# Moving the loads of w1, w2, w_out and u within batch 0 of a gated-attention and maxout kernel

## The chip, the core and the metric

The kernel runs on one core of a Trainium2 chip. The metric is device time in microseconds (us) of one execution, as the median over several runs. The engines that appear here are TensorE (PE: matmuls, with its weight loads PEld), VectorE (DVE), ScalarE (ACT), GpSimd (POOL), and SyncE (SP), which issues DMAs. All DMAs run on 16 DMA engines that are fed from two queues: the hardware queue q1, which SP issues (here nearly all transposes between SBUF tiles), and the software queue q0, which POOL issues (loads from HBM with a cast from fp32 to bf16, and the stores of the output). SBUF is the on-chip memory, PSUM the accumulators that PE writes.

## The reference

```python
def _attn_ref(u, v, z):                    # u, v: (8, 3072, 256); z: (8, 3072, 64)
    scores = (1.0 / S) * np.matmul(z, z.transpose(0, 2, 1))
    attn = np.maximum(scores, 0.0) ** 2
    out = np.matmul(attn, v)
    return (u * out).astype(np.float32)

def _moe_ref(x, w1, w2, w_out):            # x: (24576, 256); w1, w2: (256, 1024); w_out: (1024, 256)
    h1 = x @ w1
    h2 = x @ w2
    g = np.maximum(h1, h2)
    return (g @ w_out).astype(np.float32)
```

The attention output of all batches, flattened to 24576 rows, is the x of the second part. All arrays are fp32.

## The kernel before

**Tiling.** A batch has 3072 rows: 24 tiles of 128, in 6 groups of 4 tiles (512 rows). The scores of a batch are a symmetric 6 x 6 arrangement of blocks A[b, g, blk] (512 by 512, bf16). PE computes a block in two score pairs (`score_pair`, L220, two matmuls of 128 by 512 into two of the four PSUM tiles of the pool `mm_psum`); ACT applies the relu into a tile r_sb (L233, three buffers), and DVE squares it into the block (L241). A block below the diagonal is mostly not computed: it is the mirror of the one above, made by a DMA transpose that SP issues (`mirror`, L272). u is needed transposed too: `load_u` fetches 512 rows on POOL's queue (L190), `turn_u` transposes them on SP's queue (L196) into a tile uT, and `gate` multiplies the attention output by it on DVE (L434, two halves) into xT. z goes a similar way: `load_z` (L136), `turn_z` with two copies on DVE (L143) and a transpose on SP (L144).

**The second part.** max(x w1, x w2) w_out is computed as relu(x (w1 - w2)) w_out + x (w2 w_out). So DVE subtracts the weights once into w15_sb (L663), SP transposes w2 into w2T (L667), and PE multiplies w2T by w_out into W2o (L682), which needs w_out in SBUF. The function `ff` (L450, L464, L473) then does the work for a group.

**Batch 0.** Groups 0 to 3 of batch 0 run first, in the loop of L614. It walks over `steps_of(i)`, pairs (n, dc) of a key tile n (0 to 23) and a half dc of the model width; `attn_unit` (L288) issues two matmuls for each. For the first and last tiles of a group the order is all n of dc 0 and then all n of dc 1: group 3 starts so with its tiles 0 to 8, that is the blocks A[0, 3, 0], A[0, 3, 1] and the first tile of A[0, 3, 2], which are mirrors of blocks that groups 0, 1 and 2 computed. Score pairs are issued between the steps, up to 11 pairs ahead of need, one in four steps. After the fourth group come W2o, the ff of groups 0 and 1, and then groups 4 and 5 and the other batches, two groups at a time (L749 on).

**What sets the order.** The order of instructions is that of the program, per engine, within `tc.manual_schedule()`. In the loop, small conditions on (i, n) place the loads: i is the group, n the tile at which dc 0 has just been issued. A DMA on POOL's queue would run as soon as its buffer is free, so the loads here are held back: a memset of one element by DVE into the tile comes first (`held=True`, or L654 for the weights), and the DMA waits for that memset, thus for DVE's place in its own order. POOL and SP issue their DMAs strictly in order, so a DMA that waits holds up those behind it.

In the kernel before, on POOL's queue: u of group 1 is loaded at (0, 18), w2 and w1 at (1, 12), z of batch 1 at (1, 16), u of group 2 at (2, 1), w_out at (2, 4), the next z at (2, 14), u of group 3 at (3, 1). On SP's queue, in order: the mirror for group 2, the turn of u of group 1 (1, 16), the mirrors that group 3 reads first (three), the turn of z (2, 8), a mirror, w2T (2, 13), a mirror, the turn of u of group 2 (2, 16), and then the mirrors kept in the list `later` for groups 4 and 5.

Of the kernel before, what the change touches and what calls it, by code (L numbers as in the profile page):

```python
# [11 lines left out]
def kernel(  # L12
# [55 lines left out]
    def by_tile(x):  # L68
        return x.rearrange("(p t) d -> p t d", t=NT)
# [52 lines left out]
    def zT_pe(lo, n, engine):  # L122
        tp = mm_psum.tile([P, n, P], bf16, name="tpz", tag="mm")
        for j in range(n):
            nc.tensor.transpose(  # L125
                tp[:, j, :], zd_first(lo + j, 1).rearrange("p t h d -> p (t h d)"), ident
            )
        copy = nc.scalar.copy if engine == "act" else nc.vector.tensor_copy
        for k in range(0, n, G):
            copy(zT[:, lo + k : lo + k + G, :], tp[:, k : k + G, :])  # L130
# [53 lines left out]
    def load_u(b, g, held=False):  # L184
        un[b, g] = unat.tile([P, G, D], bf16, name="un")
        if held:
            nc.vector.memset(un[b, g][:, 0, 0:1], 0.0)
        step = 2 if b or g > 1 else G
        for k in range(0, G, step):
            nc.gpsimd.dma_start(  # L190
                out=un[b, g][:, ds(k, step), :], in_=by_tile(u[b])[:, ds(g * G + k, step), :]
            )

    def turn_u(b, g):
        t = upool.tile([P, G, KD, P], bf16, name="uT")
        nc.sync.dma_start_transpose(  # L196
            t.rearrange("p a c r -> p (a c) r"), un[b, g].rearrange("p a d -> p (a d)")
        )
        uT[b, g] = t
# [83 lines left out]
    def attn_unit(b, g, t, acc, dc, first, last):  # L283
        blk, j = divmod(t, G)
        a = A[b, g, blk]
        for half in range(2):
            rows = ds(half * R, R)
            nc.tensor.matmul(  # L288
                a.out(acc[half, dc]),
                v_at(b, t, dc)[rows],  # L290
                a.moving(rows, j),
                start=first,
                stop=last,
            )
        if dc == KD - 1 and j == G - 1:
            a.release()
# [4 lines left out]
    def drain(acc, dcs, copy=nc.scalar.copy):  # L301
        hs = {}
        for dc in dcs:
            hs[dc] = new_h()
            copy(hs[dc], acc[1, dc])
        for dc in dcs:
            nc.vector.tensor_add(hs[dc], hs[dc], acc[0, dc])
        return hs

    def drain_fast(acc, dc):  # L310
        hs = [new_h() for half in range(2)]
        nc.scalar.copy(hs[1], acc[1, dc])
        nc.vector.tensor_copy(hs[0], acc[0, dc])
        return hs
# [174 lines left out]
    w_out_sb = consts.tile([P, KF, D], bf16)  # L489
# [30 lines left out]
    def emit_pair(wait=0):  # L520
        nonlocal done
        early = done < 12
        finish = score_pair(
            *pairs[done], dve_half=1 if early and done % 3 == 0 else None, halves=done == 0
        )
        done += 1
        if wait:
            due.append((tick + wait, finish))
        else:
            finish()  # L530
# [10 lines left out]
    def steps_of(i):  # L541
        tiles, both = range(NT), range(KD)
        head = edge(i - 1) if i else 0
        tail = NT - edge(i)
        steps = [(n, dc) for dc in both for n in tiles[:head]]
        steps += [(n, dc) for n in tiles[head:tail] for dc in both]
        return steps + [(n, dc) for dc in both for n in tiles[tail:]]

    def pair_slots(i):
        return (  # L550
            [1, 3] + list(range(6, 40, 4)),
            list(range(3, 41, 4)),
            list(range(3, 41, 4)),
            list(range(0, 44, 4)),
        )[i]

    def need(b, g, n):
        most = pair_at[b, g, 2 * g]
        for t in range(n + 1):
            if t // G >= g:  # L560
                most = max(most, pair_at[b, g, t // 2] + 1)
        return most

    with tc.manual_schedule():
# [15 lines left out]
        w1_sb, w2_sb = (w.ap.rearrange("p (c f) -> p c f", c=KD) for w in (w1, w2))  # L580
        w2T_sb = w2T.ap.rearrange("p (c k r) -> p c k r", c=KD, r=P)

        def new_acc():
            return {
                (half, dc): acc_tile(2 * half + dc) for half in range(2) for dc in range(KD)
            }
# [27 lines left out]
        for i in range(PLAIN):  # L614
            b, g = groups[i]
            if i:
                acc = new_acc()
            new, slots = {}, pair_slots(i)
            for slot, (n, dc) in enumerate(steps_of(i)):
                tick += 1  # L620
                k = need(b, g, n)
                upto = max(k, min(done + 1, k + AHEAD)) if slot in slots else k
                while done < min(upto, len(pairs)):
                    emit_pair()
                if i == 0 and slot in (10, 22):
                    zT_pe(12 if slot == 10 else 20, 8 if slot == 10 else 4, "act")
                    if slot == 22:
                        for x in z_first:
                            x.release()
                attn_unit(b, g, n, acc, dc, n == 0, n == NT - 1)  # L630
                if n == NT - 1 and i < PLAIN - 1:
                    if i < 2:
                        new[dc] = drain_fast(acc, dc)
                    else:
                        new.update(drain(acc, [dc]))
                if dc:
                    continue
                if i in (1, 2) and n in (5, 8):
                    k = n // 8
                    nc.vector.tensor_add(sums[k][0], *sums[k])  # L640
                    sums[k] = sums[k][0]
                if i and n == 11:
                    gates = gate(*groups[i - 1], sums)
                if i and n in (11, 14):
                    gates.pop(0)()
                if i == 0 and n == 14:
                    turn_u(0, 0)
                if (i, n) in ((0, 18), (2, 1), (3, 1)):
                    load_u(0, i or 1, held=True)
                if i and n == (13 if i == 3 else 16):  # L650
                    turn_u(0, i)
                if (i, n) in ((1, 12), (2, 4)):
                    w_in = ((w2_sb, moe_w2), (w1_sb, moe_w1)) if i == 1 else ((w_out_sb, moe_w_out),)
                    nc.vector.memset(w_in[0][0][:, 0, 0:1], 0.0)  # L654
                    for w_sb, w in w_in:
                        nc.gpsimd.dma_start(
                            out=w_sb, in_=w.rearrange("(c p) f -> p c f", p=P)
                        )
                if later and n % 4 == 0 and (i == 3 or i and n > 12):
                    later.sort(key=lambda block: block[2])  # L660
                    mirror(*later.pop(0))
                if i == 2 and n == 16:
                    nc.vector.tensor_sub(w15_sb, w1_sb, w2_sb)  # L663
                    w1.release()
                    w2.release(after=COOL)
                if (i, n) == (2, 13):
                    nc.sync.dma_start_transpose(  # L667
                        w2T.ap.rearrange("p (k r) -> p k r", r=P), w2.ap
                    )
                if (i, n) in ((1, 16), (2, 14)):  # L670
                    load_z(1, i - 1, held=True)
                if (i, n) in ((2, 8), (3, 4)):
                    turn_z(1, i - 2)
                if (i, n) == (3, 5):
                    load_z(1, 2, held=True)
                if (i, n) == (3, 17):
                    turn_z(1, 2)
            if i == 3:
                for dc in range(KD):
                    ps = mm_psum.tile([P, D], fp32, name="w2o_ps", tag="mm")  # L680
                    for nb in range(KF):
                        nc.tensor.matmul(  # L682
                            ps,
                            w2T_sb[:, dc, nb, :],
                            w_out_sb[:, nb, :],
                            start=(nb == 0),
                            stop=(nb == KF - 1),
                        )
                    nc.scalar.copy(W2o_sb[:, dc, :], ps)
                w2T.release()  # L690
            sums = new
# [271 lines left out]
```

## Time and profile before

| | |
|---|---|
| median of 8 runs | 920.95 us (918.48 to 922.23) |
| the profiled execution | 919.7 us, span from first to last instruction 917.9 us |
| mean granted TensorE clock | 0.994 of full |
| DMA queues | q1 91.79 MB, 63.8% of the 16 engines' span; q0 52.58 MB, 32.1% |
| HBM | 59.77 MB read, 25.17 MB written |
| load of w1, w2 (512 KB each in SBUF) | 8.4 us median from issue to landing |
| load of w_out (512 KB) | 13.6 us |
| mirror transposes, L272 and L244 (240) | 4.9 us median |

All starts are in us from the beginning of the span. Group 0 begins near 9 us, group 3 ends at 72.7, and the W2o products start at 72.84 us. Busy time of an engine does not count the issue of DMAs. In the rows of a timeline a bracket gives the engine's idle time before the instruction and what ended it. A DMA's line on SP covers the wait for its inputs and for room in the queue, not the transfer itself. The DMA share counts the busy time of packets on the 16 engines and can exceed 1, since packets overlap on an engine.

### The profile page before, as it was taken

To read this page: it belongs to the slowest core of one execution; us is meant where nothing else is said; L and a number is where in the kernel's file an instruction comes from. 1 tells how busy PE (TensorE), PEld (TensorE's weight loads), DVE (VectorE), ACT (ScalarE), POOL (GpSimd) and SP (SyncE) were. 2 spreads that over 40 slices of the span, in tenths; PEclk is the share of its full clock that TensorE was granted. 3 is DMA by queue.
4 is the path that set the end of the run, shared out by engine and by line. 5 is a ranking of instruction groups with operands and counts; after the bars stand their busy time and mean duration, and the time that the engine had idled before them with its cause. 6 is when DMAs were issued, how large, how long until landed. Compare 5 with 4: busy or idle time off the path is not lost.

```text
span 917.9 us, 19381 instructions
## 1 busy us (share of the span) xinstructions
PE 901.4 (98%) x7478; PEld 519.8 (57%) x7526; DVE 722.6 (79%) x1097; ACT 601.8 (66%) x1192; POOL 160.8 (18%) x303
## 2 busy tenths in 40 slices
PE   9969999999999999999999999999999999999998
PEld 4426465564656655656556656466565564655655
DVE  6743699788997799977998879979799788995640
ACT  7946976667675666666766676766666667673445
POOL 3100221202202122021212022130230202101000
PEclk9979999999999999999999999999999999999999
DMA  9999999989989997999969999799989989988201
GB/s 177 129 184 195 174 188 157 189 151 168 195 157 155 164 175 154 179 147 173 195 112 207 140 175 182 133 199 145 175 174 143 186 158 175 157 158 148 78 24 70
DMA packets 396557, 145.61 MB, mean 159 GB/s; under 512 B 361904, under 2 KB 387632, under 8 KB 396464
## 3 DMA queue, kind: packets, MB, share of 16 engines
q1 hardware_dynamic: 359040, 91.79, 63.8%
q0 software_dynamic: 37424, 52.58, 32.1%
q8 instruction: 59, 0.97, 0.5%
q14 instruction: 34, 0.28, 0.1%
HBM read 59.77 MB, written 25.17 MB: 93 GB/s over the span
## 4 chain that ended last, share of the span: by engine, by line
PE 94%; DMA 4%; issue 1%; DVE 1%; ACT 0%; SPq 0%; ACTq 0%; DVEq 0%
PE acc L899 44%; PE o_ps L473 18%; PE d_ps L450 18%; PE s_ps L220 7%; PE o_ps L464 5%; DMA blk<-blk 3%; PE acc L288 2%; DMA uT<-un 1%; DVE blk L241 0%; ACT r_sb L233 0%; PE acc L592 0%; PE w2o_ps L682 0%; PE tpz L125 0%; SPq L196 0%; DVE xT L434 0%
## 5 line engine op out<-in xcount | busy, mean ns | idle before, releaser
L899 PE MATMUL acc<-blk,v_sb 64*128 64x512 bf16 x2208 | 450.4, 376 | 0.0
L233 ACT ACTIVATE r_sb<-s_ps 128x512 bf16<-128x512 f32 (+3 forms) x672 | 335.8, 558 | 132.2 <-PE s_ps L220 86.3
L899 PE MATMUL acc<-blk,vt 64*128 64x512 bf16 x1512 | 364.1, 376 | 0.0
L899 PEld LDWEIGHTS <-v_sb 64*128 64x128 bf16 x2208 | 176.2, 94 | 134.9 <-issue 5.9
L241 DVE TENSOR_TENSOR blk<-r_sb 128x1024 bf16<-128x1024 bf16 x257 | 172.3, 689 | 83.6 <-ACT r_sb L233 83.0
L457 ACT ACTIVATE g_sb<-d_ps 128x512 bf16<-128x512 f32 x384 | 193.3, 627 | 28.3 <-PE acc L899 17.8
L473 PE MATMUL o_ps<-w_out_sb,g_sb 128*128 128x256 bf16 x1536 | 175.5, 273 | 0.0
L899 PEld LDWEIGHTS <-vt 64*128 64x128 bf16 x1512 | 139.2, 94 | 62.5
L450 PE MATMUL d_ps<-xT,w_sb 128*128 128x512 bf16 x720 | 167.6, 379 | 2.6 <-issue 0.2
L473 PEld LDWEIGHTS <-g_sb 128*128 128x128 bf16 x1536 | 150.3, 98 | 17.4
L486 POOL DMA_DIRECT2D out_dram<-o_sb x88 | 48.2, 548 | 542.5 <-ACT o_sb L485 542.5
L485 ACT COPY o_sb<-o_ps 128x512 f32<-128x512 f32 (+1 forms) x98 | 56.4, 578 | 132.5 <-PE o_ps L473 132.5
L776 DVE TENSOR_TENSOR h_sb<-h_sb,acc 128x512 f32<-128x512 f32 x168 | 109.5, 683 | 28.3 <-ACT h_sb L780 20.9
L220 PE MATMUL s_ps<-zT 64*128 64x512 bf16 (+3 forms) x676 | 126.7, 360 | 0.1
L450 PEld LDWEIGHTS <-w_sb 128*128 128x128 bf16 x768 | 73.3, 98 | 89.3 <-issue 9.5
L344 DVE TENSOR_TENSOR blk<-blk,blk 128x2048 bf16<-128x2048 bf16 x63 | 77.2, 1225 | 3.0 <-DMA blk<-blk 0.9
L434 DVE SCALAR_TENSOR_TENSOR xT<-h_sb,uT 128x512 bf16<-128x512 f32 x96 | 62.0, 685 | 19.5 <-DMA uT<-un 18.1
L340 DVE TENSOR_TENSOR blk<-blk,blk 128x2048 bf16<-128x2048 bf16 x63 | 76.8, 1218 | 0.0
L791 DVE TENSOR_TENSOR blk<-blk,blk 128x2048 bf16<-128x2048 bf16 x63 | 76.6, 1219 | 0.0
L348 DVE TENSOR_TENSOR blk<-blk,blk 128x2048 bf16<-128x2048 bf16 x63 | 73.3, 1219 | 1.8 <-DMA blk<-blk 1.8
L190 POOL DMA_DIRECT2D un<-in_u_dram x94 | 50.3, 551 | 106.9 <-DMA uT<-un 82.0
L239 DVE TENSOR_TENSOR blk<-r_sb 128x512 bf16<-128x512 bf16 (+3 forms) x162 | 46.5, 324 | 20.1 <-ACT r_sb L233 19.1
(49 smaller groups left out, 360.3 us busy)
## 6 DMA issues: line engine op xcount, KB each, us to landing
out_dram<-o_sb POOLq DMA_DIRECT2D x88, 256.0 KB, 4.0
un<-in_u_dram POOLq DMA_DIRECT2D x92, 128.0 KB, 5.2
v_sb<-in_v_dram POOLq DMA_DIRECT2D x74, 128.0 KB, 5.3
blk<-blk SPq DMA_TRANSPOSE x240, 4.9
v_sb<-in_v_dram POOLq DMA_DIRECT2D x11, 256.0 KB, 8.8
zn<-in_z_dram POOLq DMA_DIRECT2D x21, 128.0 KB, 4.7
out_dram<-o_sb SPq DMA_DIRECT2D x6, 256.0 KB, 2.0
blk<-in_moe_w_dram POOLq DMA_DIRECT2D x2, 512.0 KB, 8.4
```

Source lines behind the costliest of these rows:

```text
L220: nc.tensor.matmul(s_ps[h][:, lo[h] :], zT[rows, z_at(b, blk * G + tiles[h]), :], zT[rows, q + lo[h] // P : q + G, :].rearrange("p t c -> ...
L233: nc.scalar.activation(o, s, AF.Relu)
L241: nc.vector.tensor_mul(a[:, k : k + 2, :], r, r)
L340: nc.vector.tensor_add(*alike(f["S1"], f["A21"], f["A22"]))
L344: nc.vector.tensor_sub(*alike(f["S2"], f["S1"], f["A11"]))
L348: nc.vector.tensor_sub(*alike(f["S3"], f["A11"], f["A21"]))
L450: nc.tensor.matmul(d_ps, w15_sb[:, kc, ts(nb, P)], xT[:, kc, :], start=(kc == 0), stop=(kc == KD - 1),)
L457: nc.scalar.activation(g_sb[:, nb, :], d_ps, AF.Relu)
L473: nc.tensor.matmul(o_ps[t // 2][:, t % 2, :], g_sb[:, nb, ts(t, P)], w_out_sb[:, nb, :], start=False, stop=(nb == KF - 1 and t % 2 == 1),)
L776: nc.vector.tensor_add(out, a, b_)
L791: nc.vector.tensor_sub(f["A12"].ap, f["A12"].ap, f["S2"].ap)
L899: mm = nc.tensor.matmul(a.out(acc[name]), w()[rows], a.moving(rows, j), start=name not in opened, stop=left[name] == 0,)
```

## The change

Three conditions of the loop move loads to other places. The load of u for group 1 goes from (0, 18) to (1, 8), that for group 2 from (2, 1) to (2, 5); that for group 3 stays at (3, 1). w2 and w1 go from (1, 12) to (0, 18), and w_out from (2, 4) to (2, 12). Each load takes its DVE memset along. The order of PE, ACT and SP is the same as before; on POOL the two weight loads trade places with the load of u of group 1, and the other loads keep their order.

```diff
-                if (i, n) in ((0, 18), (2, 1), (3, 1)):
-                    load_u(0, i or 1, held=True)
+                if (i, n) in ((1, 8), (2, 5), (3, 1)):
+                    load_u(0, i, held=True)
                 if i and n == (13 if i == 3 else 16):
                     turn_u(0, i)
-                if (i, n) in ((1, 12), (2, 4)):
-                    w_in = ((w2_sb, moe_w2), (w1_sb, moe_w1)) if i == 1 else ((w_out_sb, moe_w_out),)
+                if (i, n) in ((0, 18), (2, 12)):
+                    w_in = ((w2_sb, moe_w2), (w1_sb, moe_w1)) if i == 0 else ((w_out_sb, moe_w_out),)
                     nc.vector.memset(w_in[0][0][:, 0, 0:1], 0.0)
                     for w_sb, w in w_in:
                         nc.gpsimd.dma_start(
                             out=w_sb, in_=w.rearrange("(c p) f -> p c f", p=P)
                         )
```

## The prediction

> **What bounds the kernel now.** I read the page first. TensorE (PE) is busy nearly all the span, so a change off PE can only win where PE stands idle or runs at a lower clock. By stretches of 10 us, PE is full from 90 us on; the loss lies between 40 and 70 us, where batch 0 runs its third and fourth query group (columns: span, PE, PE weight loads, VectorE (DVE), ScalarE (ACT), GpSimd (POOL), each busy us and instructions; granted clock; DMA share; GB/s).
>
> ```profile
> PE 901.4 (98%) x7478; PEld 519.8 (57%) x7526; DVE 722.6 (79%) x1097; ACT 601.8 (66%) x1192; POOL 160.8 (18%) x303
> ...
> 20.00:30.00 10.00, 9.61 (x92) 5.06 (x91) 7.39 (x13) 8.69 (x17) 0.54 (x1) 1.00 0.47 67
> 30.00:40.00 10.00, 9.36 (x86) 4.61 (x84) 7.11 (x16) 8.19 (x16) 3.92 (x6) 1.00 1.05 170
> 40.00:50.00 10.00, 8.89 (x82) 4.41 (x78) 9.03 (x17) 9.42 (x19) 0.54 (x1) 1.00 1.48 136
> 50.00:60.00 10.00, 3.67 (x22) 1.40 (x24) 2.98 (x9) 2.45 (x5) 1.59 (x3) 0.71 1.33 173
> 60.00:70.00 10.00, 10.00 (x74) 4.57 (x73) 2.20 (x4) 6.49 (x12) 0.00 (x0) 0.78 1.23 206
> ```
>
> DMA is half idle at 20 to 30 us and overbooked from 40 on. PE's timeline names what it waits for: three mirrored blocks, which group 3 reads first (idle time and releaser in brackets).
>
> ```profile
> 50.33 1.04 PE L288 MATMUL acc<-blk,v_sb 64*128 64x512 bf16 x8 [1.44 <-DMA blk<-blk]
> ...
> 55.99 1.89 PE L288 MATMUL acc<-blk,v_sb 64*128 64x512 bf16 x8 [4.41 <-DMA blk<-blk]
> ...
> 59.90 1.89 PE L288 MATMUL acc<-blk,v_sb 64*128 64x512 bf16 x8 [1.59 <-DMA blk<-blk]
> ```
>
> Eight matmuls take 1.89 instead of 1.04 us there: the clock was granted at half after the longest idle time. Narrow stretches show it at 0.50 from 54.3 to 64.4 us and at 1.00 again from 64.6.
>
> ```profile
> 54.30:57.60 3.30, 1.61 (x8) 0.65 (x9) 0.50 (x3) 0.00 (x0) 0.53 (x1) 0.50 1.35 188
> ...
> 61.00:64.40 3.40, 3.40 (x18) 1.41 (x16) 0.69 (x1) 1.13 (x3) 0.00 (x0) 0.50 1.23 259
> ```
>
> So the loss on PE is 1.44 + 4.41 + 1.59 = 7.4 us of waiting, and of the clock: 56.0 to 64.5 at half speed, less 1.6 idle, is 6.9 us of work that needs 3.45: together 10.9 us. Group 3 at full clock is 96 accumulating and 22 score matmuls, two at a time at 0.2155 us (eight take four such steps, 0.86): 12.7 us, from 48.9 to 61.6 instead of 72.7. But the chain of waits shows a second chain that ends at the same place:
>
> ```profile
> 31.60 28.25 DMA blk<-blk x2
> ...
> 66.05 4.66 DMA uT<-un
> ...
> 70.80 0.10 DVE xT L434
> ...
> 71.41 0.69 DVE blk L241
> ...
> 72.19 0.61 ACT r_sb L233
> ...
> 72.84 1.91 PE w2o_ps L682 x16
> ```
>
> The transpose of u of group 2 (uT2), tenth on SP's queue since 28 us, lands at 70.71; DVE's gate waits for it, the next square, the next relu, and PE's w2o products start 2.13 us after the landing, 0.16 us after PE was free. Whoever removes only the mirrors' waits gains nothing: **uT2 has to land earlier too**.
>
> **The change part by part.** PE, ACT and SP keep their order; DVE keeps its three one-element memsets (0.06 us each) and POOL its DMA issues. What moves is when loads enter the software queue (q0), which shares the DMA engines with SP's transposes (q1).
>
> ```profile
> 20.72 0.54 POOL L190 DMA_DIRECT2D un<-in_u_dram  x1 [11.72 <-DVE un L187]
> 31.01 1.41 POOL L656 DMA_DIRECT2D blk<-in_moe_w_dram  x2 [9.75 <-DVE blk L654]
> ...
> 39.05 0.89 POOL L656 DMA_DIRECT2D w_out_sb<-in_moe_w_out_dram  x1 [1.25 <-DVE w_out_sb L654]
> ```
>
> *w1 and w2 go from 31.0 to 20.7 us.* At 31 they land 7.2 and 9.6 us after issue, and of the 1.54 MB that DMA moves from 33 to 42.4 us the transposes get 0.22: the first mirror, issued at 31.60, lands at 50.28. At 20.7 only uT0 is on q1, landed at 21.4; u took 3.6 us there for 256 KB, so 1024 KB land by about 28 and hold up nobody: the next transpose issue ends at 30.2. The edit costs nothing; were that cover gone, it would delay that one mirror, which PE first reads at 36.9.
>
> *u of group 1 goes from 20.7 to about 29.0* (its memset now follows the addition that ends at 28.9). Alone 3.6 us, beside the mirror that lands at 32.60 some 5: it lands at 33 to 34. SP's uT1, issued at 30.3 until now, waits for that, and behind it in order stand the three mirrors, which start near 35 instead of 31.6. Without w1 and w2 beside them they land, at the 2.4 us that consecutive mirrors are apart from 61 to 68 us (63.22, 65.66, 68.03), near 40, 43 and, with u2 beside it, at most 49. PE wants them at 48.9, 50.0 and 51.0. uT1 itself lands near 38; its gate stands at 43.96. Price on PE: nothing, with 2 us of margin at the tightest.
>
> *u of group 2 goes from 36.7 to about 39.5*, two issues of 0.54 us. uT2 is only reached after eight other transposes: nothing. u of group 3 stays.
>
> *w_out goes from 39.05 to about 45.5* (DVE's first gate half of group 2 ends at 44.65, one square follows, then the memset). This is the edit with a price, because w_out is now ahead of a small load that DVE waits for soon. In the trace w_out lands at 52.69; u before it on q0 landed at 45.42, so its service took 7.3 us. z, issued at 46.76, followed at 55.75, 3.06 us later, and DVE waited for it, while PE stood idle anyhow:
>
> ```profile
> 55.84 0.49 DVE L143 COPY zd<-zn 128x512 bf16<-128x512 bf16 x2 [2.42 <-DMA zn<-in_z_dram]
> ```
>
> After the change w_out's packets start at about 46.8 (u's began about 1.3 us after its issue at 20.72), so w_out ends near 54.3 and z near 57.4. DVE's copy is in order at group 3's fifth tile, and the squares of later score pairs stand behind it. PE can go on for five pairs: three buffers of r_sb, and two pairs of the four PSUM tiles. At one pair in 1.08 us the first pair behind the copy is issued at 50.9 and the sixth at 56.2; from z's landing to a free PSUM tile are 0.5 (copies) + 0.7 (square) + 0.6 (relu) = 1.8 us. So z is in time until 54.4, and PE **loses about 3 us** at 56. Bounds: 0 if w_out is served at the 0.13 MB/us of the w loads' stretch (landing before 51), 8 if it takes its whole 13.6 us again.
>
> *When does uT2 land?* By megabytes left at 46.8 us. Before, q1 moved 3.37 MB from there to 70.7, q0 0.89; the last stretch, with q0 empty, ran at 0.198 MB/us:
>
> ```profile
> q1 hardware_dynamic: 13404, 3.37, 99.6%
> q0 software_dynamic: 1298, 0.89, 31.5%
> ```
> ```profile
> q1 hardware_dynamic: 7315, 1.84, 120.0%
> ```
>
> After, q1 still has w2T and two mirrors (3 x 0.524), uT2 (0.262), zT and half of the third early mirror (0.50): 2.34 MB, a lead of 1.03 MB, worth 5.2 us at 0.198. Against it q0 still has all of w_out, two z and u3, 1.05 MB, or 0.16 more; at w_out's 0.067 MB/us (0.49 in 7.3 us) the shared stretch lasts 2.4 us longer, in which q1 runs at some 0.08 to 0.13 instead of 0.198: 0.2 MB, 1.0 us. **uT2 lands 4.2 us earlier, at 66.5**, and w2o starts at 68.6. Bounds: 58.6 if q1 is not slowed at all (2.34 / 0.198 = 11.8), then 61.6 on PE decides and the whole 10.9 is won; 73.1 if all 3.39 MB run at 0.129, the pace of 45.4 to 52.7. I take 66.5: the mean pace over 46.8 to 70.7, 0.179, gives 65.7.
>
> *The clock.* PE is done with group 3 at 61.6 + 3 = 64.6 and idles 4 us before w2o. In the trace a stretch of 3.4 us with 0.7 us of work in it (from 50.8) ended at half speed, and stretches half filled kept it there. If it falls in the first idle time, near 57, the half speed is spent mostly in work that has to wait for uT2: about nothing. If it falls in the second, w2o and the ff products run at half for 3.4 to 6.8 us, a loss of 1.7 to 3.4. Halved between the two: **1.2 us**.
>
> Sum: 4.2 - 1.2 = **3.0 us less**. The z wait is inside it, since uT2 ends later. After 72 us everything moves with PE: uT3 and the later mirrors follow uT2 on q1, 4 us earlier, and PE has no wait over 0.2 us to give back.
>
> The Trainium skill weighs in twice. Its page "TensorE: Matmul & The Clock Gate" (Part 1, and the section on HAM oscillation) says that PE falls to half speed after an idle window of about 3.4 us, and to avoid gaps longer than that. The row above is a stricter case: the longest gap was 4.41 us, but the clock fell 2.7 us into it. By the rule the 3 us gap would be free and the 4 us gap decisive, and the sum 1.8 instead of 3.0. Its page "DMA: Bandwidth & Descriptors" (Anatomy of one DMA) fits a load on this path as 2.0 us plus bytes over 436e3 per us: 4.4 us for w_out's 1.05 MB in HBM, where the row has 13.6. By the rule the z wait and the 1.0 us of shared queue vanish, and 5.2 us are won.
>
> **The rivals.** (a) *The whole wait goes.* If w_out and the transposes share better once w1 and w2 are gone, uT2 lands by 62 and 8 to 10.9 us are won: about 911. For it: with u3 and z beside them, from 52.7 to 61.4, DMA moved 188 GB/s, not 129. Against: w_out and z are all in this stretch now.
> (b) *w_out takes the place of w1 and w2.* uT2 lands at 69 to 70, 1 to 2 us are won and the clock takes them back: 920 to 922. For it: the bytes of q0 in front of uT2 shrink only by w1 and w2 less u1.
> (c) *Slower: w_out starves the queue, then the clock.* If DMA moves less than 0.145 MB/us from 46.8 on (3.39 / 0.145 = 23.4), uT2 lands after 70.2; PE idles some 6 us or more ahead of w2o, and half speed in w2o and ff costs 1.7 to 3.4 where before it was hidden behind the same landing. Net +2 to +3.7: 923.7. For it: 0.129 was the pace while w_out was served. Against: 188 and 200 after it.
> (d) *It doesn't do what it says*: the u1 load comes too late and mirror waits remain. Against: 8 us between the first mirror's landing and its use. Counted in (b).
>
> **How the numbers follow.** The profiled execution took 919.7 us (span 917.9); the median of the eight is 920.95, 1.25 above. Less 3.0 that is 916.7 for the profile, **918.0 for the median**. Chances: forecast 0.55 (its own range 915 to 920.5), (a) 0.17, (b) with (d) 0.15, (c) 0.13. The eight runs spread from 918.48 to 922.23, 0.2% either way, so no change means 919.1 to 922.8. Of the forecast 0.12 lies above 919.1. Faster 0.43 + 0.17 = 0.60; within 0.2% 0.12 + 0.13 = 0.25; slower 0.13 + 0.02 = 0.15. The range 911.5 to 921.8 cuts half of (a)'s tail, and (c).
>
> **What would show it.** Right: the w loads at 20.7 us land before 29; the waits for blk at 48 to 60 us are gone; DVE's zd copy waits about 6 us, then its gate for uT near 66; PE idles near 56 and before w2o; w2o starts near 68.6. Wrong: PE waits for a mirror again in group 3; w_out lands before 51; uT2 before 62 or after 70; w2o with no idle ahead of it; or a new wait past 90 us.

## The result and the profile after

The changed kernel takes 916.62 us in the median of 22 runs (914.01 to 922.07), the kernel before 921.19 us in the median of the 62 that stand beside it (917.38 to 929.86). The ratio is 0.9952, with a 95% interval of 0.9939 to 0.9964: about 4.6 us faster. The profiled execution of the changed kernel took 917.72 us, with a span of 914.9 and a mean granted clock of 0.996; before it was 919.7 and 917.9. The spans differ by 3.0 us only, because this execution lost 1.4 us within its first 9 us, in a place that the change doesn't touch (last section). To compare places, starts below are also given *aligned*: shifted so that the second half of the first gate (L434) starts at 29.41 us, as in the profile before. It starts at 30.80 after, so 1.39 is taken off.

The page and the stretches of 10 us of the changed kernel (columns as in the prediction):

```profile
PE 899.5 (98%) x7478; PEld 519.6 (57%) x7526; DVE 724.4 (79%) x1097; ACT 602.0 (66%) x1192; POOL 160.2 (18%) x303
```
```profile
20.00:30.00 10.00, 9.61 (x90) 4.99 (x88) 6.99 (x12) 8.69 (x16) 1.42 (x2) 1.00 0.80 141
30.00:40.00 10.00, 9.36 (x85) 4.61 (x82) 7.15 (x14) 8.19 (x17) 1.08 (x2) 1.00 0.99 144
40.00:50.00 10.00, 10.00 (x95) 5.19 (x91) 9.36 (x20) 9.51 (x19) 2.49 (x4) 1.00 1.16 171
50.00:60.00 10.00, 9.72 (x90) 4.93 (x89) 6.03 (x13) 9.67 (x19) 1.58 (x3) 1.00 1.30 225
60.00:70.00 10.00, 6.13 (x46) 3.53 (x42) 4.84 (x10) 2.97 (x7) 0.00 (x0) 0.79 1.14 198
70.00:80.00 10.00, 9.73 (x61) 6.37 (x62) 2.25 (x4) 5.57 (x11) 0.55 (x1) 0.87 1.12 208
```

From 50 to 60 us, where PE was busy for 3.67 us before, it is now busy for 9.72 at full clock. The loss has moved to 60 to 73 us and has become smaller. The loads stand in the new places (POOL's timeline; in brackets the idle time before the issue and what ended it):

```profile
22.11 1.42 POOL L656 DMA_DIRECT2D blk<-in_moe_w_dram  x2 [13.81 <-DVE blk L654]
30.59 0.54 POOL L190 DMA_DIRECT2D un<-in_u_dram  x1 [7.07 <-DVE un L187]
...
46.49 0.89 POOL L656 DMA_DIRECT2D w_out_sb<-in_moe_w_out_dram  x1 [4.39 <-DVE w_out_sb L654]
47.69 0.54 POOL L136 DMA_DIRECT2D zn<-in_z_dram  x1 [0.31 <-DVE zn L135]
```

The w loads land at 27.65 and 30.14, u of group 1 at 35.90, w_out at 53.14 and z at 54.06. DVE waited 0.68 us for that z, and PE not at all. PE's own timeline shows what is left:

```profile
52.78 1.04 PE L288 MATMUL acc<-blk,v_sb 64*128 64x512 bf16 x8
...
67.19 3.57 PE L682 MATMUL w2o_ps<-w_out_sb,blk 128*128 128x256 bf16 x16 [3.87 <-ACT r_sb L233]
```

The eight matmuls that read the third mirror take 1.04 us and have no wait of note ahead of them. The waits for mirrors (7.4 us) have gone; the only gap left in this part is 3.87 us in front of the w2o products. The chain of waits names its source (start, us, what):

```profile
42.30 10.44 DMA blk<-blk
52.74 0.04 issue
52.78 1.04 PE acc L288 x8
...
61.75 3.31 DMA uT<-un
...
65.16 0.10 DVE xT L434
...
65.77 0.69 DVE blk L241
...
66.54 0.60 ACT r_sb L233
```

It is the prediction's second chain: uT2 lands at 65.06, aligned 63.67, which is 7.0 us earlier than before, and the w2o products start 2.13 us after it, as before. In that gap the clock falls. Narrow stretches just before w2o, in it and behind it:

```profile
63.40:67.10 3.70, 0.00 (x0) 0.00 (x0) 1.94 (x4) 0.56 (x2) 0.00 (x0) 0.82 1.13 209
67.20:72.50 5.30, 5.08 (x20) 3.04 (x21) 5.05 (x10) 2.75 (x6) 0.00 (x0) 0.50 1.14 212
72.70:76.10 3.40, 3.40 (x22) 1.98 (x21) 0.00 (x0) 3.40 (x7) 0.00 (x0) 1.00 1.14 212
```

The records of the clock have it at 0.50 from 65.75 to 72.58. From the start of w2o to the first matmul of groups 4 and 5 it is 20.11 us (67.19 to 87.30), where before it was 17.48 (72.84 to 90.32): the fallen clock costs 2.63. So the account closes: w2o 7.04 earlier, less 2.63, is 4.41 us, and the medians differ by 4.57.

### The profile page after: what moved, and what is told of

Same layout as the page of the kernel before. It is cut to its first block, busy times and chain, and to the rows that moved or that the text cites. A ratio compares the mean times of both kernels' runs of the same rounds, so it can differ in the third digit from the quotient of the medians.

```text
span 914.9 us, 19382 instructions
## 1 busy us (share of the span) xinstructions
PE 899.5 (98%) x7478; PEld 519.6 (57%) x7526; DVE 724.4 (79%) x1097; ACT 602.0 (66%) x1192; POOL 160.2 (18%) x303
## 4 chain that ended last, share of the span: by engine, by line
PE 96%; DMA 2%; DVE 1%; issue 1%; ACT 0%; ACTq 0%; DVEq 0%; SPq 0%
PE acc L899 44%; PE o_ps L473 18%; PE d_ps L450 18%; PE s_ps L220 7%; PE o_ps L464 5%; PE acc L288 3%; DMA blk<-blk 1%; PE w2o_ps L682 0%; DMA uT<-un 0%; ACT r_sb L233 0%; DVE blk L239 0%; DVE blk L241 0%; PE acc L592 0%; PE tpz L125 0%; DVE zT L130 0%
## 5 line engine op out<-in xcount | busy, mean ns | idle before, releaser
L450 PEld LDWEIGHTS <-w_sb 128*128 128x128 bf16 x768 | 73.6, 98 | 90.2 <-issue 10.9
L434 DVE SCALAR_TENSOR_TENSOR xT<-h_sb,uT 128x512 bf16<-128x512 f32 x96 | 62.0, 684 | 20.4 <-DMA uT<-un 19.0
L239 DVE TENSOR_TENSOR blk<-r_sb 128x512 bf16<-128x512 bf16 (+3 forms) x162 | 48.4, 336 | 20.1 <-ACT r_sb L233 19.1
```

The costliest lines, as they stand in the source:

```text
L450: nc.tensor.matmul(d_ps, w15_sb[:, kc, ts(nb, P)], xT[:, kc, :], start=(kc == 0), stop=(kc == KD - 1),)
```

## The experiments

Each kernel was timed beside runs of the kernel before on the same chip. Columns: median, median of before beside it, ratio with its 95% interval, and from the profile, aligned, where uT2 lands, where w2o starts and where groups 4 and 5 start. Each profile is one execution, each median 5 to 12 runs (22 for the change).

| kernel | median | before | ratio | uT2 | w2o | groups 4, 5 |
|---|---|---|---|---|---|---|
| before | - | - | 1 | 70.71 | 72.84 | 90.32 |
| the change | 916.62 | 921.19 | 0.9952 [0.9939, 0.9964] | 63.67 | 65.80 | 85.91 |
| e1, only w1 and w2 | 914.69 | 920.71 | 0.9932 [0.9910, 0.9955] | 63.60 | 65.73 | 85.93 |
| e2, only w_out | 917.08 | 920.71 | 0.9961 [0.9941, 0.9981] | 66.33 | 68.46 | 85.94 |
| e3, only u | 926.63 | 920.71 | 1.0055 [1.0035, 1.0076] | 75.48 | 77.61 | 95.08 |
| e4, earlier turn of u of group 2 | 915.41 | 920.71 | 0.9947 [0.9924, 0.9970] | 61.51 | 63.64 | 81.12 |
| e5, all w, not u | 916.84 | 921.97 | 0.9949 [0.9929, 0.9969] | 64.46 | 66.59 | 86.48 |
| e6, clock kept | 915.12 | 921.97 | 0.9929 [0.9903, 0.9955] | 64.44 | 66.57 | 84.05 |
| e7, both turns earlier | 911.50 | 921.97 | 0.9892 [0.9870, 0.9913] | 58.72 | 61.84 | 79.33 |
| e8, e1 and both turns | 913.03 | 921.97 | 0.9903 [0.9873, 0.9933] | 57.22 | 61.62 | 79.11 |
| e9, e7 and w2T earlier | 910.81 | 921.18 | 0.9910 [0.9878, 0.9942] | 60.46 | 62.59 | 80.07 |
| e10, w2T earlier | 912.60 | 921.18 | 0.9912 [0.9896, 0.9928] | 62.69 | 64.82 | 83.62 |
| e11, w_out earlier | 914.57 | 921.18 | 0.9933 [0.9919, 0.9947] | 64.02 | 66.15 | 85.97 |
| e12, e9 and w_out earlier | 914.10 | 921.18 | 0.9931 [0.9911, 0.9951] | 62.43 | 64.56 | 83.71 |

### Which part of the change does it

**e1**, against the kernel before: only w1 and w2 move.

```diff
-                if (i, n) in ((1, 12), (2, 4)):
-                    w_in = ((w2_sb, moe_w2), (w1_sb, moe_w1)) if i == 1 else ((w_out_sb, moe_w_out),)
+                if (i, n) in ((0, 18), (2, 4)):
+                    w_in = ((w2_sb, moe_w2), (w1_sb, moe_w1)) if i == 0 else ((w_out_sb, moe_w_out),)
```

> Only w1 and w2 move to (0, 18), behind the load of u of group 1; w_out stays at (2, 4) and u as before. Theory (w1 and w2 delayed the mirrors and, by the bytes in front of it, uT2): the mirror waits of 7.4 us in group 3 are gone or under 1 us, uT2 lands 5 to 7 us earlier than before, and 3 to 5 us are won: 916 to 918. Rival (the gain needs w_out out of the mirrors' way too): the mirrors still meet w_out, PE still waits 3 us or more for blk in group 3, and the time stays at 920 to 921.

914.69 us, a little better than expected. The three mirrors land at 39.19, 42.52 and 50.70, PE's waits for them are gone, it idles 4.04 us before w2o, and the clock is at half from 65.86 to 72.69: and uT2, w2o and groups 4 and 5 come where the full change has them, to 0.1 us. **The move of w1 and w2 alone is enough for the whole gain.**

**e2**, against the kernel before: only w_out moves, `(2, 4)` to `(2, 12)` in the same two lines.

> Only w_out moves to (2, 12); w1 and w2 stay at (1, 12). Theory (uT2's landing decides, and the same bytes lie in front of it): the mirror waits shrink, from 7.4 to some 3 us, but uT2 lands within 1 us of before and w2o starts there: 920 to 922, no gain. Rival (the mirror waits decide): the waits that shrink are won, 916 to 918.

917.08 us: my theory fell, since the gain is 3.6 us and uT2 lands 4.4 us earlier, although it still has the same bytes in front of it. Waits for a mirror remain, but they have shrunk from 7.4 to 3.3 us. PE's timeline of e2:

```profile
50.52 1.04 PE L288 MATMUL acc<-blk,v_sb 64*128 64x512 bf16 x8 [0.36 <-DVE h_sb L307]
...
56.19 1.89 PE L288 MATMUL acc<-blk,v_sb 64*128 64x512 bf16 x8 [3.34 <-DMA blk<-blk]
...
69.83 1.91 PE L682 MATMUL w2o_ps<-w_out_sb,blk 128*128 128x256 bf16 x16 [1.80 <-ACT r_sb L233]
```

With w_out out of the way behind w1 and w2, the first mirror lands at 47.03 (aligned 45.66, before 50.28), and what follows moves up. The DMA views from 46 to 56 us show the same two kinds of work at a different pace, first before, then e2:

```profile
DMA packets 4449, 1.44 MB, mean 144 GB/s; under 512 B 3489, under 2 KB 4448, under 8 KB 4448
```
```profile
DMA packets 6188, 1.93 MB, mean 193 GB/s; under 512 B 5035, under 2 KB 6187, under 8 KB 6187
```

At the aligned place, from 47.37 to 57.37 us, e2 has 186. So the pace, and not only the bytes, depends on what stands behind what. Why the engines moved 144 in the one and 186 in the other isn't settled here.

Groups 4 and 5 start at 85.94 in e2, the same as in e1 and in the change: it keeps a mirror wait of 3.34 us and a stretch at half speed there, but has only 1.80 us of idle time ahead of w2o and no fall of the clock in it. So w_out alone reaches the same place in another way, and the gains of the parts don't add up.

**e3**, against the kernel before: only u moves, the first two lines of the change's diff.

> Only the loads of u move: group 1 to (1, 8), group 2 to (2, 5). Theory: 256 KB more lie in front of the mirrors while DMA is full, so uT2 and w2o come 1 to 3 us later: 922 to 924. Rival (the place of u is free, it is only 256 KB): 920.5 to 921.5.

926.63 us: slower, as expected, but twice as much. u of group 1 lands at 35.04, so its turn and the mirrors behind it on SP meet w1 and w2. PE's timeline of e3:

```profile
55.03 1.49 PE L288 MATMUL acc<-blk,v_sb 64*128 64x512 bf16 x8 [4.88 <-DMA blk<-blk]
...
63.29 1.89 PE L288 MATMUL acc<-blk,v_sb 64*128 64x512 bf16 x8 [6.34 <-DMA blk<-blk]
...
66.48 1.89 PE L288 MATMUL acc<-blk,v_sb 64*128 64x512 bf16 x8 [0.86 <-DMA blk<-blk]
```

12.1 us of waits instead of 7.4, and half clock from 55.48 to 69.13. The late u is harmless only because w1 and w2 have made room for it.

**e5**, against the changed kernel: the loads of u stand as before (the first two lines of the change's diff undone).

> w1, w2 and w_out as in the changed kernel, u of groups 1 and 2 loaded where it was before, so only the u part is undone. Theory (with w1 and w2 out of the way the later load of u costs SP's queue 3 to 4 us at uT1, since the three mirrors stand behind it, but they have that time): the first mirror issues near 33 instead of 37, uT2 lands 1 to 3 us earlier than after the change, and the time is 1 to 3 us below the changed kernel: 913.5 to 915.5. Rival (the load of u at (1, 8) costs as much here as alone, 5.9 us): 910.5 to 911.5. Rival (once the w loads are away its place is free): 916 to 917.

916.84 us, the last rival's figure: at a ratio of 0.9949 it is as good as the change's 0.9952, and the 1 to 3 us of the theory didn't come. The mirrors land earlier (37.94, 41.42, 46.91), but uT2 does not (64.46 aligned against 63.67). With w1 and w2 early, the places of u and of w_out add nothing that can be measured.

### What the rest of the wait is

**e4**, against the changed kernel: u of group 2 is turned at (2, 10), before w2T and a mirror instead of behind them.

```diff
-                if i and n == (13 if i == 3 else 16):
+                if i and n == (0, 16, 10, 13)[i]:
                     turn_u(0, i)
```

> The changed kernel, and on SP's queue the turn of u of group 2 goes from (2, 16) to (2, 10), ahead of w2T and one mirror; nothing else moves. Theory (after the change uT2 is what PE waits for ahead of w2o, 3.9 us, and the half clock after it costs 2.7 more): uT2 lands near 60, PE idles under 1.5 us there, the clock stays whole, and it is 4 to 6.5 us faster than the changed kernel: 910 to 912.5. Rival (the mirrors' removal was the whole gain, the wait for uT2 is slack, or w2T takes its place): 915 to 917.

w2o starts 2.16 us earlier than in the changed kernel, the gap is 1.60 us, the clock holds, and groups 4 and 5 start 4.8 us earlier. Yet the median is 915.41, hardly better than the change and in the rival's range, not in that of the theory. The wait was not slack, though: the lead was lost again later. DVE's and PE's timelines of e4 show where the rest went:

```profile
88.06 1.29 DVE L434 SCALAR_TENSOR_TENSOR xT<-h_sb,uT 128x512 bf16<-128x512 f32 x2 [19.36 <-DMA uT<-un]
```
```profile
63.64 1.91 PE L682 MATMUL w2o_ps<-w_out_sb,blk 128*128 128x256 bf16 x16 [1.60 <-ACT r_sb L233]
...
90.71 0.93 PE L220 MATMUL s_ps<-zT 64*128 64x512 bf16 x2 [3.37 <-ACT r_sb L233]
```

The next transposed u (uT3) now comes too late for the earlier group 4: DVE's gate waits for it, squares and relus stand behind the gate, PE waits 3.37 us and the clock falls once more (91.37 to 94.78). The gain had become a new wait, one group further on.

**e7**, against e4: the u of group 3 is turned earlier too, at (3, 5).

```diff
-                if i and n == (0, 16, 10, 13)[i]:
+                if i and n == (0, 16, 10, 5)[i]:
```

> e4_turn_early, and the turn of u of group 3 goes from (3, 13) to (3, 5), ahead of one more mirror and z's transpose. Theory (in e4 the wait went on to the next u: DVE's gate stood for uT3 until 88.0 us, the squares of groups 4 and 5's score pairs behind it, and PE lost 3.4 us and 1.7 of clock at 90.7): that wait is gone, and it is 3 to 5 us below e4: 910 to 912.5. Rival (another transpose, the mirror behind it, is then the one that PE waits for): 914 to 916.

911.50 us, as expected: 0.9892. The stretches from 50 to 70 us of e7:

```profile
50.00:60.00 10.00, 10.00 (x96) 5.30 (x94) 5.88 (x14) 8.71 (x18) 1.59 (x3) 1.00 1.39 229
60.00:70.00 10.00, 9.80 (x75) 6.73 (x73) 5.20 (x10) 6.91 (x15) 0.00 (x0) 1.00 1.08 212
```

PE is full, the clock never falls until the end of the span, PE has no wait over 0.4 us from 10 to 140 us, and groups 4 and 5 start 11.0 us earlier than before (79.33 against 90.32). That is the 10.9 us which the prediction read off as lost in group 3; the median gives 10.5 of it.

**e8**: e1 with both early turns, so u loads and w_out as before.

> The kernel before with w1 and w2 at (0, 18) (e1_w_only), and both turns of u early as in e7. Theory (uT2's wait of 4.0 us and the clock's 2.6 are what e1 still loses): 908.5 to 911, the fastest of all. Rival (w_out at (2, 4) delays the third mirror or uT2 as much as it saves): 911 to 914.

913.03 us, 2 us more than expected and in the rival's range; but neither the third mirror nor uT2 was late. Through batch 0 its profile is as good as e7's (groups 4 and 5 at 79.11). The profiled execution then lost time in later batches: PE waited 0.89 us at 137 and 2.52 us at 174 us, places where e7's didn't wait. Why is not shown. The intervals of e7 and e8 overlap, so that w_out or u in the new places are worth something beside early turns is not shown.

**e6**, against the changed kernel: 14 more matmuls at the end of group 3, with a weight tile of zeros, just before its last unit, so that PE works through most of the wait.

```diff
+        zero = consts.tile([P, P], bf16, name="zero")
+        nc.gpsimd.memset(zero, 0.0)
...
+                for _ in range(14 if (i, n, dc) == (3, NT - 1, 1) else 0):
+                    nc.tensor.matmul(
+                        acc[0, 1],
+                        zero,
+                        w_out_sb[:, 0:2, :].rearrange("p c f -> p (c f)"),
+                        start=False,
+                        stop=False,
+                    )
```

> The changed kernel with 14 more matmuls of 512 columns at the end of group 3 that add zero (weights of zero, w_out as the moving side), 3.0 us of work put into the idle time ahead of w2o. Theory (the clock falls there because of PE's idle time, and that costs 2.6 us in w2o and ff): no stretch at half speed near w2o, from w2o's start to the first matmul of groups 4 and 5 17.5 us instead of 20.1, w2o no more than 0.5 us later, and 1 to 2.6 us below the changed kernel in the median: 914 to 915.6. Rival (the loss is not the clock's, or adding zero work only moves w2o): 916.5 to 919.

915.12 us, as expected. PE's timeline of e6, and the stretch that answers to the half-clock one of the changed kernel:

```profile
61.76 3.20 PE L633 MATMUL acc<-w_out_sb,zero 128*128 128x512 bf16 x13
...
66.93 1.91 PE L692 MATMUL w2o_ps<-w_out_sb,blk 128*128 128x256 bf16 x16 [1.65 <-ACT r_sb L233]
```
```profile
67.00:72.30 5.30, 5.30 (x34) 3.20 (x34) 5.00 (x10) 4.98 (x12) 0.00 (x0) 1.00 1.12 210
```

34 matmuls instead of 20 fit into 5.3 us, the clock is whole, and from w2o to groups 4 and 5 it is 17.48 us again instead of 20.11. That measures the clock's part by itself: 2.63 us. w2o starts 0.77 us later than in the changed kernel, because uT2 lands as much later, where 0.5 was allowed. The medians don't resolve the gain: 0.9929 against 0.9952 for the change and 0.9949 for e5 beside it, with intervals that overlap.

### What is ahead of uT2 on the queues

**e10**, against the changed kernel: SP issues w2T at (1, 10) instead of (2, 13), one transpose of 512 KB less ahead of uT2.

```diff
-                if (i, n) == (2, 13):
+                if (i, n) == (1, 10):
                     nc.sync.dma_start_transpose(
```

> The changed kernel with the transpose of w2 alone moved to (1, 10). Theory (what stands ahead of uT2 on SP's queue sets its landing): 0.52 MB less ahead of it after 47 us, uT2 lands about 2 us earlier than after the change, w2o starts 2 us earlier, and the idle time ahead of it falls to some 2 us, so that the half clock comes less often: 2 to 4 us below the changed kernel: 912.5 to 914.5. Rival (the transpose only moves the work to ahead of the mirrors, and uT2 lands where it did): 916 to 918.

912.60 us, as expected; the interval (0.9896 to 0.9928) lies below the change's. uT2 lands 1.0 us earlier (2 were expected), the gap is 3.13 us, and the clock falls for 3.41 us instead of 6.83: from w2o to groups 4 and 5 18.80 us. The smaller gap gives more through the clock (1.3 us) than through itself. In three of its five executions the mean granted clock was 1.000, in the changed kernel's 22 in one, so the fall came less often too.

**e9**: e7 with the same early w2T.

> e7_turns_early, and the transpose of w2 goes from (2, 13) to (1, 10), where SP otherwise waits for u of group 1. Theory (in e7 w2T lands at 61.08 and PE starts on it at 61.13, the third mirror comes 0.6 us before its use, so small delays in other executions reach PE): w2T lands before 40, the other transposes of the first 60 us come 2 us earlier or are unmoved, and it is the same as e7 or up to 2 us faster, with less spread: 909.5 to 911.5. Rival (0.5 MB more ahead of the three mirrors makes PE wait for the third one): 912.5 to 915.

910.81 us, at 0.9910 the same as e7 within the intervals: once uT2 is early enough, nothing is left for w2T to give in this place. The spread did not shrink (909.37 to 919.39). The three mirrors, which now stand behind w2T, land 1.1 to 5.6 us later than in e7 (aligned), and the profiled execution waits 0.70 us for the third.

**e11**, against the changed kernel: w_out is loaded at (1, 10), so its bytes are gone long before uT2.

```diff
-                if (i, n) in ((0, 18), (2, 12)):
+                if (i, n) in ((0, 18), (1, 10)):
```

> The changed kernel with w_out loaded at (1, 10), behind u of group 1, instead of (2, 12). Theory (while w_out is served the transposes nearly stop, so it should be served when none is urgent): w_out lands before 42, z at 47.7 lands within 4 us, DVE's copy of z no longer waits, uT2 lands 3 to 5 us earlier, and it is 3 to 5 us below the changed kernel: 911.5 to 913.5. Rival (it now stops the first mirrors, and PE waits 2 us or more for blk in group 3, as before the change): 917 to 921.

914.57 us, 1 us above the expected range. w_out lands at 37.86, DVE's wait for z is gone and PE has no wait for a mirror; but uT2 lands at 64.02 aligned, no earlier than in the changed kernel. From 52 to 60 us, aligned, DMA moved 0.81 MB of transposes and 0.39 of loads, in the changed kernel 1.35 and 0.40, and SP was at the issue of one mirror from 52.52 to 59.46, while u of group 3 was being loaded (landed at 59.17). So bytes taken out in front did not come back as time, because the pace fell with them. Why it fell stays open.

**e12**: e9 with the early w_out.

> e9_turns_w2T and w_out at (1, 10) as in e11. Theory (PE has no wait over 0.4 us left between 12 and 140 us, so only the spread shrinks): 908.5 to 911. Rival (w2T and w_out together, 1 MB more in q0 and q1 ahead of the three mirrors, bring PE's wait for blk back): 913 to 918.

914.10 us, the rival's side. Four things now share the queue between 30 and 45 us; w_out lands at 41.03, w2T at 43.90, the turn of u of group 1 at 45.49, PE waits 0.56 us in group 3 and 2.00 us before w2o, and the clock falls once. Early is not free: what is moved forward meets what was there.

## Why the prediction was right, point by point

- **The two chains** that end together, the mirrors' and uT2's: right, and the core of it. With the mirrors' waits gone, PE ended group 3 10.75 us earlier (63.32 less 1.39, against 72.68) and then stood waiting for uT2. e7 shows the rest by undoing it: with uT2 early enough the whole 10.9 us are there.
- **w1 and w2 cost nothing at 20.7 us**: right; e1 shows that this edit alone carries the gain.
- **u of group 1**: no price on PE, as predicted, but the margin was mis-sized. The mirrors were to land near 40, 43 and at most 49; they landed, aligned, at 40.24, 44.12 and 51.35, and PE lost some 0.23 us at the third (0.45 instead of 0.22 us between the tiles). The prediction let the three follow one another from 35 on; but DVE finishes the square that completes the third one's block only at 42.28 (40.89 aligned), SP begins it at 42.30, in e1 as well although SP had been free there since 39.28, and from there it took 10.44 us to land. e3 shows the same edit without the cover that was named for it.
- **w_out, 7.3 us of service, and 3 us on PE for z**: mis-sized. w_out's packets began 2.9 us after its issue at 46.49, not 1.3, but were then served faster: they run from 49.36 to 52.78, 0.52 MB at 0.153 MB per us and not 0.067. z landed 0.9 us after w_out, not 3.06. Aligned, that was at 52.67, in time for the 54.4 that the prediction had worked out, so PE lost nothing and DVE's copy waited 0.68 us, not about 6. It did not touch the sum, since the z wait lay inside the wait for uT2.
- **uT2 4.2 us earlier**: 7.0. The bytes were about right (3.39 MB from 46.8 us on were expected, 3.66 went from 48.2 to 65.1, the same place aligned). The pace was not: 3.66 in 16.9 us is 0.217 MB per us, where 3.39 in the 19.7 us of the forecast is 0.172. The prediction let the stretch shared with w_out last as long as the old one, 7.3 us and more, with the transposes at 0.08 to 0.13 MB per us in it. In fact they nearly stopped (q0 moved 0.65 MB and q1 0.11 from 49.2 to 53.2 us), but for about half as long.
- **The clock, 1.2 us**: 2.63, shown by e6. The prediction halved between falling in an early gap, for free, and falling before w2o, for 1.7 to 3.4. As z did not make PE wait, there was no early gap, and the upper half of that bound came true.
- **Sum**: -7.0 + 2.6 = -4.4 instead of -4.2 + 1.2 = -3.0. Both mis-sized terms pull against each other: an earlier uT2, and a clock that falls where it costs. The mechanism held; that the sum came within 1.4 us, with terms off by 2.8 and 1.4, is in part luck.
- **Rivals**: (a), the whole wait goes, needs uT2 by 62; the change alone does not reach it, e7 does, at 911.50 where (a) said about 911. (b) would have had uT2 at 69 to 70, and the part of it that e2 tested, no gain while the same bytes stand in front, fell. (c) needed a pace below 0.145 MB per us; it was 0.217. (d) is left as 0.23 us.

The Trainium skill's page "TensorE: Matmul & The Clock Gate" (Part 1, What's actually happening, and HAM oscillation) describes a free-running window of about 3.4 us, a fall after an idle one, and a rule against gaps longer than that. The windows agree: every stretch at half speed was 3.41, 6.83, 10.24 or 13.65 us long, but for the last one of each profile, which the end of the record cuts. The length of gap in the rule does not bound the fall here: gaps of 3.13 us (e10) and 2.00 us (e12) were enough (last section).

## What to carry to other kernels

When a wait is taken off the bounding engine, look for the next thing that ended at the same time, and move that in the same edit: here it was a transpose tenth in its queue, and behind it the same transpose of the next group (e4, then e7), and only with both turns did the 10.9 us come that the waits had shown. Try each part of such a change alone, since here either of two parts brought the gain or most of it without the other, and the third was a loss by itself. Price a gap on TensorE as the gap and the clock that falls in it: 3.87 us of idle time cost 2.63 more, and how much it costs depends on where the gap lies (last section).

## What was not expected of the hardware

**How the clock falls and comes back.** The length of a gap doesn't decide it: 2.00 us of idle time (e12) brought half speed, 2.52 us (e8, from 173.90 to 176.42) did not. The starts of the stretches at half speed, the one at the end of the work included, lie whole numbers of 3.413 us apart in every profile that has two (in the change 65.75 and 915.67, 249 such windows), so the windows stand at fixed places. What fits every profile is the time that PE is busy within one window. The last window before the fall of e12, a later window of e12 without a fall, and the two windows into which the gap of e8 is split (columns as in the prediction: behind the comma stands PE's busy time, then those of PEld, DVE, ACT and POOL, the granted clock, the DMA share and GB/s):

```profile
62.77:66.18 3.41, 1.41 (x15) 0.67 (x12) 2.26 (x4) 0.87 (x2) 0.00 (x0) 1.00 1.24 269
```
```profile
909.28:912.69 3.41, 1.45 (x14) 1.06 (x11) 0.00 (x0) 0.97 (x3) 0.00 (x0) 1.00 0.36 129
```
```profile
172.16:175.57 3.41, 1.74 (x18) 0.85 (x15) 3.17 (x5) 0.55 (x2) 1.62 (x4) 1.00 1.23 248
175.57:178.98 3.41, 2.33 (x21) 1.28 (x22) 3.41 (x7) 0.18 (x1) 0.49 (x1) 1.00 1.13 170
```

In the fourteen profiles the clock fell after each of the 15 full-speed windows in which PE was idle for 2.00 us or more, and after none in which it was idle for 1.96 or less (counted from 5 us on to the window in which PE's work ends). It came back after a window at half speed with at most 0.75 us idle (0.67 in e10, 0.74 in e2), and stayed at half for another after one with 1.10 or more (1.25 in e1, 1.44 in the change, 2.01 in e11). So the price of a gap depends on where it lies in the window: the 3.87 us of the change had 2.43 before the boundary and 1.44 behind it, and cost two windows; the 3.13 us of e10 had 2.46 and 0.67, and cost one.

**A pause of the DMA engines with work outstanding.** The DMA view of the changed kernel from 46 to 56 us, in slices of 0.25 us (busy tenths, then GB/s):

```profile
DMA  9970100899999999999999999999999999999999
GB/s 233 87 27 8 12 4 12 92 219 289 288 292 291 255 199 195 190 197 182 160 154 160 191 197 208 179 190 207 153 205 139 201 276 287 206 249 292 289 290 292
```

From 46.50 to 47.75 us almost nothing moves, although the second half of u had not landed (48.32) and SP was at the issue of the third mirror from 42.30 to 47.89. The profile before has such a stretch from 48.25 to 49.50, with w_out issued and not landed, and e1 and e2 have one too. In e1 the transposes also got next to nothing while w_out was served (queue, packets, MB and share in the stretch from 42.6 to 46.4 us), though SP was at the issue of a mirror from 42.30 to 47.32:

```profile
q0 software_dynamic: 1010, 0.51, 114.0%
q1 hardware_dynamic: 71, 0.02, 2.2%
```

Other than the section on the profile before says, a line of SP here does not include the wait for the inputs: this one begins at 42.30, when DVE had finished the block at 42.28, and the turn of u of group 1 in the change begins at 35.97, after its u had landed at 35.90. In e5, where the last load of u had landed at 42.01 and w_out was issued only at 45.45, the issue of the same mirror took 1.96 us (41.27 to 43.23). So the transposes seem to be held at their issue, while loads are outstanding, rather than on the engines; what holds them was not found.

**A start that is sometimes 1.4 us late.** In some of the profiles the second square of DVE (L239) takes 2.5 us instead of 0.4 to 0.6, and ends with GpSimd's six casts (L120) that began beside it. DVE and POOL in the changed kernel's profile, then in e7's:

```profile
5.73 2.85 DVE L239 TENSOR_TENSOR blk<-r_sb 128x512 bf16<-128x512 bf16 x2
...
6.16 2.14 POOL L120 CAST blk<-z 128x256 bf16<-128x256 f32 x6
```
```profile
5.73 0.75 DVE L239 TENSOR_TENSOR blk<-r_sb 128x512 bf16<-128x512 bf16 x2
...
6.16 3.21 POOL L120 CAST blk<-z 128x256 bf16<-128x256 f32 x6
```

One of the two engines is held up: DVE, and PE then waits 2.2 us at 8.97, or POOL, whose casts take 1.07 us longer and delay nobody. Six of the fourteen profiles had the first. The Trainium skill's page "SBUF — State Buffer" (SBUF: two separate sides) says that a VectorE operation with two SBUF inputs and a GpSimd operation that reads SBUF share a port pair, which the one that starts first holds for its whole instruction. The rows fit a lock, but not that rule to the letter: DVE's second square started at 6.06, before the first cast at 6.16, and was held through all six. That the port is the cause is argued, not tested. The 1.4 us can be a part of the spread from run to run; how often they come outside the profiles is not shown.
